# Single gate/value steps in token halves, quarter outputs copied by VectorE, and a bare group ahead of its score units, in an attention and SwiGLU kernel

## The chip, the core and the metric

The kernel runs on one core of a Trainium2 chip. The core has a matmul engine (TensorE, PE in the profile, with its weight loads shown as PEld), a vector engine (VectorE, DVE), an activation engine (ScalarE, ACT), a general engine (GpSimd, POOL) and a queue engine (SyncE, SP). They run in parallel, each works through its own list of instructions in order, and they wait for one another with semaphores. Matmul results go to PSUM, which has eight banks of 512 float32 columns in each of 128 partitions; everything else lives in SBUF. The metric is the device time of one execution in microseconds. The kernel before takes 429.18 us (median of three runs, 428.72 to 429.24).

## What is computed

Multi-head softmax attention over 8 batches, 12 heads, 448 tokens and 64 elements per head, then a gated feed-forward block over the 3584 resulting tokens:

```python
scores = scale * np.matmul(q, k.transpose(0, 1, 3, 2))
scores = scores - np.max(scores, axis=-1, keepdims=True)
attn = np.exp(scores)
attn = attn / (np.sum(attn, axis=-1, keepdims=True) + 1e-09)
out = np.matmul(attn, v)
...
g = x @ w_gate                              # 768 -> 1536
silu = g * (1.0 / (1.0 + np.exp(-g)))
val = x @ w_val                             # 768 -> 1536
return (silu * val @ w_out)                 # 1536 -> 768
```

Inputs and the output are float32; the matmuls run in float16.

## The kernel before

**Attention.** Two heads make a pair (48 pairs, six per batch). The scores of a pair come in units: a unit is a pair of score products for a slab of up to 128 keys against 448 queries, one product per head, in one PSUM tile `s` of two banks (`qk_quad`, L356 and L368), and one exponential on ScalarE that takes both heads from PSUM to SBUF (`exp`, L378, 128x896). From pair 12 on, a pair has three units of 128 keys and shares a fourth unit, which holds the 64 leftover keys of two pairs, with its neighbour. The weighted sums of values (L462, `acc`) take 8 matmuls that read the leftover keys (`pv_rest`, 64 rows) and 24 that read 128 keys (`pv_piece`), twelve for each head of the pair; each head has an `acc` tile of its own. VectorE closes a head with a reciprocal (L504) and a product (L505, `xt`); DMA transposes (L555, L561) then put the result into the feed-forward input `X`.

**Feed-forward.** Tokens go through it in blocks of 384 or 512. One *step* computes 128 of the 1536 inner columns for a block: six gate matmuls into `gp`, six value matmuls into `vp` (both L615), on ScalarE a tanh (L642, `sg`), on VectorE `t = (sg + 1) * gp` (L670) and `hts = t * vp` (L676). Outputs of a block come in *groups* (`OutPair.wide`, seven products of six matmuls, L734, with sums made beforehand by VectorE at L598 to L601) or, for what a group can't take, in *quarter outputs* (`plain_out`: twelve matmuls of 192 columns, L710, and a copy from PSUM at L717). The last two token blocks of 896 use another scheme (L888, L1082, L734), from about 278 us to the end.

**The order by hand.** The program is written in visits: a list `plan` gives each visit three score units and, in most visits, one pair whose values are due (`todo`). From the visit numbered `base` on, the table `VISITS` says what feed-forward work joins: (begins a block, steps, groups, quarter outputs, sums). A visit without `todo` is called bare. Visits with one step and a pair due (`lone`) are the *single steps*; there are seventeen of them, eight with 384 tokens and nine with 512. Their order on TensorE is: three score units, the eight leftover-key matmuls, the twelve of head 0 (`pv_side(p0, 0)`), the gate's six matmuls, the twelve of head 1, six value matmuls for the first half of the tokens, six for the second half. Visits with two steps, groups or quarter outputs stand between them. In single steps of 384 tokens the exponential of the third unit is held back (`late_exp`) until the tanh has been queued.

**PSUM.** Two pools use all eight banks. `ps_s` has three slots of two banks, tag "s": score tiles, the gate's tile, the group's `og` and some small outputs. `ps_f` has two slots of one bank, tag "f": `acc`, `vp`, `op`, `ob`. A new tile gets the slot that was released first, and its first matmul waits until the last reader of the old tile is done. In a single step of before, the gate's result `gp` is one bank of a `ps_s` tile, and the other bank (`self.spare`) takes the value product of the first token half; that of the second half is a `ps_f` tile. The slot is thus held until L676 has read the first half:

```python
gs = ps_s.tile([128, 2, 512], FP32, tag="s", name="gp")
gp, self.spare = gs[:, 0], gs[:, 1]
...
dst = ps_f.tile([128, 512], FP32, tag="f", name="vp") if half else self.spare
```

**Around the change.** In the last visits (`VISITS` entries 25 to 32) four quarter outputs, two groups and the sums of tokens and weights for the last scheme (`token_sums`, L1071 to L1074; `weight_sums`, L851 to L854 on GpSimd) are spread over the visits. The second of these groups falls into the bare visit (entry 31); there, two score units come ahead of the group and the third between its products.

Of the kernel before, what the change touches and what calls it, by code (L numbers as in the profile page):

```python
# [10 lines left out]
FP32 = mybir.dt.float32  # L11
# [54 lines left out]
def kernel(  # L66
# [410 lines left out]
    def pv_piece(pr, c, hx, first=False, last=True):  # L477
        for j in range(KR + 1):
            pv_mm(pr, hx, c, j, accs[pr][hx], first and c + j == 0, last and c == KR - 1 and j == KR)
# [19 lines left out]
    def pv_close(pr, hx):  # L499
        e_done(pr, hx)  # L500
        xt = Xts[pr % NX].rearrange("p (s h) d -> p s h d", h=2)
        a4 = accs[pr][hx][:, 0 : (KR + 1) * (D + 1)].rearrange("p (s d) -> p s d", s=KR + 1)
        r = attp.tile([128, KR + 1], FP32, tag="R", bufs=4, name="R")
        nc.vector.reciprocal(r[:], a4[:, :, D])  # L504
        nc.vector.tensor_tensor(  # L505
            xt[:, :, hx],
            a4[:, :, 0:D],
            r[:].unsqueeze(2).to_broadcast([128, KR + 1, D]),
            ALU.mult,
        )  # L510
# [3 lines left out]
            for c in range(KR):  # L514
                pv_piece(pr, c, hx)

    def pv_side(pr, hx):
        for c in range(KR):
            pv_piece(pr, c, hx)
        pv_close(pr, hx)  # L520

    def pv_quad(pr):
        pv_pieces(pr)
        if pr == XPE:
# [79 lines left out]
    class Step:  # L604
# [42 lines left out]
        def value(self, half):  # L647
# [14 lines left out]
                self.vp = ps_f.tile([128, 512], FP32, tag="f", name="vp")  # L662
            self.group("v", self.vp, range(half * NCB // 2, (half + 1) * NCB // 2))

        def gated(self):
            if self.t1 is None:
                n = self.at[2]
                self.t1 = fp.tile([128, 512], FP32, tag="t1", name="t1")
                self.readers.append(
                    nc.vector.scalar_tensor_tensor(  # L670
                        self.t1[:, 0:n], self.sg[:, 0:n], 1.0, self.gp[:, 0:n], ALU.add, ALU.mult
                    )
                )
# [12 lines left out]
    def store(osb, kk, l0, n, m0, w, queues=(nc.sync,), large_first=False):  # L686
# [12 lines left out]
        for x, (_, dst, src) in enumerate(parts):  # L699
            queues[x % len(queues)].dma_start(dst, src)  # L700

    def plain_out(kk, c0, hts, ch, m0, w, osb):
        if out_small[0]:
            out_small[0] = False
            op = ps_s.tile([128, 2, 512], FP32, tag="s", name="op")[:, 0]
        else:
            op = ps_f.tile([128, 512], FP32, tag="f", name="op")
        oh, off = divmod(m0, OH)
        for fb in range(NFB):
            nc.tensor.matmul(  # L710
                op[:, 0:w],
                lhsT=hts[:, fb, ts(ch, 128)],
                rhs=wo[oh][:, fb, ds(off, w)],
                start=fb == 0,
                stop=fb == NFB - 1,
            )
        nc.scalar.activation(osb[:, ds(m0, w)], op[:, 0:w], AF.Copy, scale=1.0 / HS)  # L717
        if m0 + w == DM:
            store(osb, kk, c0 + ch * 128, 128, 0, DM)

# [19 lines left out]
    def apart(mms, *others):  # L740
        for mm in mms:
            for other in others:
                tc.declare_no_dep(mm.ins, other.ins, reason="another bank")

    class OutPair:
# [29 lines left out]
        def wide(self, keep, add_sum, ns=(1, 2, 1), units=()):  # L775
            osb = self.open()
            g = ps_s.tile([128, 2, 512], FP32, tag="s", name="og")
            a, c = g[:, 0, 0:OH], g[:, 1, 0:OH]
            if self.last:
                bs = ps_s.tile([128, 2, 512], FP32, tag="s", name="ob")  # L780
                parts = [(i * QW, QW, bs[:, i, 0:QW]) for i in range(2)]
            else:
                parts = [(0, OH, ps_f.tile([128, 512], FP32, tag="f", name="ob")[:, 0:OH])]
            p1, p15 = (k[:, 0:OH] for k in keep)
            both = (nc.sync, nc.scalar)

            def products(lhs, m, first=False):
                return [(lo, w, b, product(b, lhs, self.tt(m, lo, w), first)) for lo, w, b in parts]

            def combine(dst, x, scale, y, lo, w):  # L790
                return nc.vector.scalar_tensor_tensor(  # L791
                    dst[:, ds(lo, w)], x[:, ds(lo, w)] if scale == HS else x, scale, y, ALU.mult, ALU.add
                )

            product(a, self.hh(0, self.x), self.bb(0, 0, 0, OH), True)
            keep1 = nc.scalar.activation(p1, a, AF.Copy, scale=1.0 / HS)
            apart(product(c, self.hh(0, self.y), self.tt(0, 0, OH), True), keep1)
            for unit in units:
                qk(*unit)
            done = [nc.vector.scalar_tensor_tensor(p15, c, 1.0 / HS, p1, ALU.mult, ALU.add)]  # L800
            for lo, w, b, mms in products(self.hs(0), 1, True):
                done.append(combine(c, p15, HS, b, lo, w))
            add_sum(ns[0])
            apart(product(a, self.hh(1, self.x), self.bb(0, 1, 0, OH)), *done)
            left = nc.scalar.activation(osb[0][:, 0:OH], a, AF.Copy, scale=1.0 / HS)
            for one in done[1:]:
                tc.declare_no_dep(left.ins, one.ins, reason="another bank")
            if self.last:
                self.stored(0, 0, OH, both)
            for lo, w, b, mms in products(self.hs(1), 2):  # L810
                combine(osb[1][:, OH:], b, 1.0 / HS, p15[:, ds(lo, w)], lo, w)
            if self.last:
                self.stored(1, OH, OH, both)
            add_sum(ns[1])
            apart(product(c, self.hs(2), self.bb(1, 1, 0, OH)), left)
            nc.scalar.activation(osb[0][:, OH:], c, AF.Copy, scale=1.0 / HS)
            if self.last:
                self.stored(0, OH, OH, both)
            else:
                self.stored(0)  # L820
            ends = []
            for lo, w, b in parts:
                mms = product(b, self.hh(1, self.y), self.tt(3, lo, w))
                apart(mms, *ends)
                ends.append(combine(osb[1], b, 1.0 / HS, p1[:, ds(lo, w)], lo, w))
                if self.last:
                    self.stored(1, lo, w, both)
            if not self.last:
                self.stored(1)
            add_sum(ns[2])  # L830
# [146 lines left out]
    with tc.manual_schedule():  # L977
# [50 lines left out]
        def add_block(i, visits):  # L1028
# [36 lines left out]
        ]  # L1065

        def token_sums(x, w, t, eng=nc.vector):
# [54 lines left out]
        def run_steps(n):  # L1122
            for _ in range(n - 2):
                run_fv()
            if n > 1:
                run_pair()
            elif n:
                run_fv()
# [109 lines left out]
        for x, (chunks, todo) in enumerate(plan):  # L1238
# [12 lines left out]
            lone = nf == 1 and bool(todo) and not split  # L1251
            behind = []
            for n, (pr, c) in enumerate(ordered if x else []):
                if n == 2 and ng and not todo:
                    behind.append((pr, c, small))
                    continue
                if n == 2 and ordered[n] in quads:
                    rests = open_products(rests, small)
                late = n == 2 and not todo and c < NC and pr < QUAD and bool(fvq) and not fvq[0].at[1]
                late = late or n == 2 and lone and not fvq[0].at[1]  # L1260
                qk(pr, c, small, late)
# [29 lines left out]
            for _, p0 in todo:  # L1291
                if split:
                    pv_split(p0)
                elif lone:
                    step = fvq.pop(0)
                    step.split = step.alone = True
                    gate_small[0] = False
                    pv_side(p0, 0)
                    step.gate()
                    pv_side(p0, 1)  # L1300
                else:
                    pv(p0)
                if p0 < XPE:
                    turns.append(p0)
                elif fvq and fvq[0].at[0] < p0 // NHP // NB - 1:
                    held.append(p0)
                else:
                    turn_x(p0)
# [25 lines left out]
            else:  # L1334
# [3 lines left out]
                for _ in range(ng):  # L1338
                    run_group(behind)
                if lone:  # L1340
                    step.gated()
                    step.value(0)
                    step.finish()
                    add_sum()
                elif bare_next(x):
                    for _ in range(nf):
                        run_fv()
                else:
                    run_steps(nf)
                for _ in range(no):  # L1350
                    run_o()
                    out_small[0] = True
# [159 lines left out]
```

## Time and profile before

The profiled execution took 428.64 us; its span from first to last instruction is 426.9 us. A visit of the single-step stage lasts 4.0 us (384 tokens) or 4.6 us (512).

| stretch (us) | what runs | length | PE busy | DVE busy | ACT busy | POOL busy |
|---|---|---|---|---|---|---|
| 123.50 to 245.10 | all single steps, with groups and two-step visits | 121.60 | 119.48 | 73.86 | 78.10 | 92.19 |
| 245.10 to 277.90 | visits with quarter outputs and groups, to the end of attention | 32.80 | 31.95 | 23.87 | 23.56 | 12.98 |
| whole span | | 426.9 | 418.5 | 265.4 | 247.5 | 224.3 |

The granted TensorE clock is 0.999 of full speed over the run. A busy PE is not PE at its peak: a matmul's row lasts from its start to its modelled end, some 0.15 to 0.2 us after the next one can start, so that short waits between matmuls hide under the tails of earlier rows. They are seen in the distance between the starts of rows that do the same work.

### The profile page before, as it was taken

The page shows a single profiled execution, that of the slowest core. Times are in us where ns is not written, and L with a number is a line of the kernel's source. Part 1 is how long each engine was busy: PE and PEld are TensorE (multiplying, and loading weights), DVE is VectorE, ACT ScalarE, POOL GpSimd, SP SyncE. Part 2 cuts the span into 40 slices and gives each one's busy share as a digit, 9 for nine tenths or more (in the row PEclk, how much of TensorE's full clock was granted, in tenths as well). Part 3 has the DMA queues.
Part 4 walks back from the last instruction along what each step waited for, and adds up shares of the span by engine and source line. Part 5 has one row for each costly group of instructions (what it writes and reads, how often), then busy time and mean ns, then how long its engine had stood idle before and what let it go on. Part 6 is the DMA issues. An engine that isn't in the chain of part 4 may idle for free.

```text
span 426.9 us, 10560 instructions
## 1 busy us (share of the span) xinstructions
PE 418.5 (98%) x4226; PEld 251.1 (59%) x4226; DVE 265.4 (62%) x592; ACT 247.5 (58%) x371; POOL 224.3 (53%) x343
## 2 busy tenths in 40 slices
PE   8999999999999999999999999999999999999996
PEld 3666666655556666675666577555555655555564
DVE  4667562786677664567655576665656575575563
ACT  6976667646767574766656677655543225545221
POOL 8656625987998777486967723599900000000000
PEclk9999999999999999999999999999999999999999
DMA  9999999999999999999999928410000331000125
GB/s 134 191 200 200 199 175 189 130 178 190 181 175 135 155 202 174 134 165 148 128 142 173 113 55 139 126 52 0 2 0 20 92 98 53 2 0 0 38 74 149
DMA packets 108465, 50.26 MB, mean 118 GB/s; under 512 B 60416, under 2 KB 105344, under 8 KB 108416
## 3 DMA queue, kind: packets, MB, share of 16 engines
q0 software_dynamic: 46800, 24.56, 48.4%
q1 hardware_dynamic: 61344, 24.79, 32.3%
q8 instruction: 33, 0.54, 0.5%
q10 hardware_dynamic: 272, 0.25, 0.2%
q14 instruction: 16, 0.13, 0.1%
HBM read 49.55 MB, written 11.01 MB: 142 GB/s over the span
## 4 chain that ended last, share of the span: by engine, by line
PE 90%; DVE 6%; ACT 2%; issue 1%; DVEq 0%; ACTq 0%
PE gp L615 15%; PE un L888 13%; PE og L734 10%; PE ub L888 10%; PE acc L462 8%; PE ob L734 8%; PE vp L615 7%; PE s L356 5%; PE op L710 4%; PE s L393 2%; PE acc L426 2%; DVE t L670 2%; PE op L1082 2%; DVE hts L676 2%; DVE xt L505 1%; PE tp L324 1%
## 5 line engine op out<-in xcount | busy, mean ns | idle before, releaser
L378 ACT ACTIVATE E<-s 128x896 f16<-128x896 f32 x126 | 107.4, 918 | 40.4 <-PE s L356 28.9
L615 PE MATMUL gp<-X,wg 128*128 128x384 f16 (+1 forms) x288 | 61.4, 353 | 0.1
L240 POOL COPY qk<-qkraw 128x512 f16<-128x512 f16 x70 | 43.6, 668 | 28.3 <-DMA qkT<-qk 25.4
L180 POOL DMA_DIRECT2D vraw<-in_v_dram x72 | 44.1, 634 | 14.6 <-DMA wo<-in_moe_w_out_dram 7.8
L615 PE MATMUL vp<-X,wv 128*128 128x384 f16 (+3 forms) x288 | 48.7, 305 | 0.0
L615 PEld LDWEIGHTS <-wv 128*128 128x128 f16 x432 | 39.5, 98 | 15.4
L462 PEld LDWEIGHTS <-E 128*128 128x128 f16 (+2 forms) x1224 | 40.3, 98 | 13.3 <-issue 5.4
L462 PE MATMUL acc<-vo,E 128*128 128x65 f16 (+2 forms) x1224 | 46.2, 193 | 0.6 <-DVE osb L791 0.3
L180 POOL DMA_DIRECT2D qkraw<-in_k_dram x70 | 42.5, 624 | 5.3 <-DMA wo<-in_moe_w_out_dram 3.4
L403 ACT ACTIVATE E<-s 112x896 f16<-112x896 f32 x48 | 40.7, 917 | 7.7 <-PE s L393 7.7
L670 DVE SCALAR_TENSOR_TENSOR t<-sg,gp 128x384 f32<-128x384 f32 (+1 forms) x48 | 29.4, 617 | 24.1 <-ACT sg L642 24.1
L615 PEld LDWEIGHTS <-wg 128*128 128x128 f16 x288 | 25.9, 97 | 21.8 <-issue 1.7
L734 PEld LDWEIGHTS <-hts 128*128 128x128 f16 x270 | 26.0, 98 | 16.6 <-issue 0.6
L642 ACT ACTIVATE sg<-gp 128x384 f32<-128x384 f32 (+1 forms) x48 | 26.0, 547 | 15.4 <-PE gp L615 13.7
L356 PE MATMUL s<-qkT 64*64 64x448 f16 (+1 forms) x288 | 31.7, 355 | 1.9 <-DVE hts L676 1.3
L505 DVE TENSOR_TENSOR xt<-acc,R 128x256 f16<-128x256 f32 x72 | 30.6, 425 | 2.5
L203 POOL DMA_DIRECT2D qkraw<-in_q_dram x43 | 29.4, 683 | 5.0 <-DMA vraw<-in_v_dram 2.0
L504 DVE RECIPROCAL R<-acc 128x4 f32<-128x4 f32 x72 | 12.9, 179 | 27.9 <-PE acc L462 27.7
L676 DVE SCALAR_TENSOR_TENSOR hts<-t,vp 128x384 f16<-128x384 f32 (+3 forms) x48 | 23.9, 499 | 3.0 <-PE vp L615 1.2
L953 ACT ACTIVATE silu<-un 128x448 f32<-128x448 f32 x24 | 13.0, 543 | 21.9 <-PE un L888 19.6
L937 DVE TENSOR_TENSOR un<-ub,kept 128x448 f32<-128x448 f32 x24 | 15.1, 631 | 16.6 <-ACT kept L934 10.3
L734 PE MATMUL og<-wo,hts 128*128 128x384 f16 x132 | 25.0, 326 | 0.4 <-ACT E L378 0.4
(207 smaller groups left out, 735.4 us busy)
## 6 DMA issues: line engine op xcount, KB each, us to landing
vraw<-in_v_dram POOLq DMA_DIRECT2D x72, 64.0 KB, 5.0
qkraw<-in_q_dram POOLq DMA_DIRECT2D x39, 112.0 KB, 4.6
qkraw<-in_k_dram POOLq DMA_DIRECT2D x68, 64.0 KB, 4.8
wg<-in_moe_w_gate_dram POOLq DMA_DIRECT2D x8, 288.0 KB, 10.0
wv<-in_moe_w_val_dram POOLq DMA_DIRECT2D x8, 288.0 KB, 10.5
wo<-in_moe_w_out_dram POOLq DMA_DIRECT2D x2, 1152.0 KB, 17.9
out_dram<-osb SPq DMA_DIRECT2D x7, 288.0 KB, 3.5
out_dram<-osb SPq DMA_DIRECT2D x9, 192.0 KB, 3.4
```

The lines of the kernel that those rows point to most:

```text
L180: eng.dma_start(dst[ts(s, 64)], rows)
L240: nc.gpsimd.tensor_copy(dst.rearrange("p c h d -> p h c d"), src)
L356: nc.tensor.matmul(s[ts(half, m), hx, 0:S].rearrange("p (c q) -> p c q", q=P), lhsT=t[ts(hx, 64), ds((c + low(pr, hx)) * 128 + half * m, m ...
L378: nc.scalar.activation(e, s[:, :, 0:S], AF.Exp, scale=sm_scale)
L403: nc.scalar.activation(e[:, :, 0:S], s[0:P, :, 0:S], AF.Exp, scale=sm_scale)
L462: nc.tensor.matmul(acc[ds(lo, m), ts((j + pr % 2) % (KR + 1), D + 1)], lhsT=e[rows, ds(hx * S + j * 128 + lo, m)], rhs=Vts[pr % NV][rows, ...
L505: nc.vector.tensor_tensor(xt[:, :, hx], a4[:, :, 0:D], r[:].unsqueeze(2).to_broadcast([128, KR + 1, D]), ALU.mult,)
L615: nc.tensor.matmul(dst[:, 0:w], lhsT=wslice(kind, self.fb, cb), rhs=X[kk][:, cb, ds(c0 + lo, w)], start=(cb == 0), stop=(cb == NCB - 1),)
L670: nc.vector.scalar_tensor_tensor(self.t1[:, 0:n], self.sg[:, 0:n], 1.0, self.gp[:, 0:n], ALU.add, ALU.mult)
L676: nc.vector.scalar_tensor_tensor(self.hts[:, self.fb, ds(lo, w)], self.t1[:, ds(lo, w)], 0.5 * HS, vp[:, 0:w], ALU.mult, ALU.mult)
L734: nc.tensor.matmul(dst, lhsT=lhs(n), rhs=rhs(n), start=first and n == 0, stop=n == NH - 1, skip_group_check=True)
L888: mm = nc.tensor.matmul(dst, lhsT=lhs[:, n], rhs=rhs[:, n], start=first and n == 0, stop=n == NK - 1, skip_group_check=True,)
```

## The change

Four things change.

1. Single steps run in a new method `halves`. The pair's values are finished first (`pv`, both heads, then both closings). Then the gate runs as two groups of six matmuls, one per token half, each in a bank of its own of one `ps_s` tile; each half has its own tanh and its own `t`. The held-back exponential is queued after both. The two value halves get a `ps_f` tile each, and `hts` is made from the two after both products. `pv_side` goes.
2. In quarter outputs from `base` on, VectorE copies the result from PSUM instead of ScalarE.
3. In a bare visit with a group, all three score units are handed to the group: its first two products come ahead of the first two units, and the third follows after the fourth product.
4. The table's last rows move: quarter outputs in entries 25, 26, 27 and 29 instead of 25, 26, 28 and 29; the group of entry 27 goes to entry 28; the sums ask for 1, 1, 2, 0, 1, 1 in entries 25 to 30 instead of 2, 2, 0, 2, 0, 0.

```diff
+        def halves(self):
+            w = self.at[2] // 2
+            parts = [ds(i * w, w) for i in range(2)]
+            gs = ps_s.tile([128, 2, 512], FP32, tag="s", name="gp")
+            self.sg = fp.tile([128, 512], FP32, tag="sg", name="sg")
+            self.t1 = fp.tile([128, 512], FP32, tag="t1", name="t1")
+            readers = []
+            for i, part in enumerate(parts):
+                g = gs[:, i, 0:w]
+                apart(self.group("g", gs[:, i], range(NCB), (i * w, w)), *readers)
+                readers.append(nc.scalar.activation(self.sg[:, part], g, AF.Tanh, scale=0.5))
+                readers.append(
+                    nc.vector.scalar_tensor_tensor(self.t1[:, part], self.sg[:, part], 1.0, g, ALU.add, ALU.mult)
+                )
+            while late_exp:
+                late_exp.pop(0)()
+            vps = [ps_f.tile([128, 512], FP32, tag="f", name="vp") for _ in parts]
+            for i, vp in enumerate(vps):
+                self.group("v", vp, range(NCB), (i * w, w))
+            for i, vp in enumerate(vps):
+                self.close(i * w, w, vp)
...
-        nc.scalar.activation(osb[:, ds(m0, w)], op[:, 0:w], AF.Copy, scale=1.0 / HS)
+        if by_vector[0]:
+            nc.vector.tensor_scalar_mul(osb[:, ds(m0, w)], op[:, 0:w], 1.0 / HS)
+        else:
+            nc.scalar.activation(osb[:, ds(m0, w)], op[:, 0:w], AF.Copy, scale=1.0 / HS)
...
-            for unit in units:
+            for unit in units[:2]:
                 qk(*unit)
...
+            for unit in units[2:]:
+                qk(*unit)
             for lo, w, b, mms in products(self.hs(1), 2):
...
-            (4, 0, 0, 1, 2), (0, 0, 0, 1, 2), (0, 0, 1, 0, 0), (0, 0, 0, 1, 2), (0, 0, 0, 1, 0),
-            (0, 0, 0, 0, 0), (0, 0, 1, 0, 0), (0, 0, 0, 0, 0),
+            (4, 0, 0, 1, 1), (0, 0, 0, 1, 1), (0, 0, 0, 1, 2), (0, 0, 1, 0, 0), (0, 0, 0, 1, 1),
+            (0, 0, 0, 0, 1), (0, 0, 1, 0, 0), (0, 0, 0, 0, 0),
...
-                if n == 2 and ng and not todo:
+                if ng and not todo:
                     behind.append((pr, c, small))
                     continue
...
-                elif lone:
-                    step = fvq.pop(0)
-                    step.split = step.alone = True
-                    gate_small[0] = False
-                    pv_side(p0, 0)
-                    step.gate()
-                    pv_side(p0, 1)
                 else:
                     pv(p0)
...
                 if lone:
-                    step.gated()
-                    step.value(0)
-                    step.finish()
+                    fvq.pop(0).halves()
                     add_sum()
...
+                by_vector[0] = True
                 for _ in range(no):
                     run_o()
```

More of the change, by code (lines that the diff above doesn't have):

```diff
@@ L515, in pv_pieces @@
                 pv_piece(pr, c, hx)
[L517 to L520, printed above, removed]
     def pv_quad(pr):
@@ L700, in store @@
             queues[x % len(queues)].dma_start(dst, src)
+    by_vector = [False]
     def plain_out(kk, c0, hts, ch, m0, w, osb):
```

## The prediction

> **What bounds the kernel now.** I first read the page for the busy shares. TensorE (PE) is busy nearly all the time, so only PE's waits can be won and only what makes PE wait can lose.
>
> ```profile
> PE 418.5 (98%) x4226; PEld 251.1 (59%) x4226; DVE 265.4 (62%) x592; ACT 247.5 (58%) x371; POOL 224.3 (53%) x343
> ```
>
> Next the stretches: in the stage of single steps the other engines have room (columns: stretch, length, then busy us of PE, PEld, DVE, ACT, POOL).
>
> ```profile
> 123.50:245.10 121.60, 119.48 (x1445) 77.52 (x1444) 73.86 (x197) 78.10 (x106) 92.19 (x154) 1.00 1.21 151
> ```
>
> Then the timeline of PE alone. A row's duration runs past the start of the next matmul, so I read distances between starts. First a visit behind a two-step visit, then single steps of 384 (from 183.28) and 512 tokens (191.97).
>
> ```profile
> 137.16 0.74 PE L356 MATMUL s<-qkT 64*128 64x448 f16 x6
> 137.74 0.76 PE L462 MATMUL acc<-vo,E 64*128 64x65 f16 x20
> 138.53 1.14 PE L615 MATMUL gp<-X,wg 128*128 128x384 f16 x6
> ...
> 183.28 0.55 PE L356 MATMUL s<-qkT 64*128 64x448 f16 x4
> 184.01 0.36 PE L356 MATMUL s<-qkT 64*128 64x448 f16 x2 [0.18 <-DVE hts L676]
> 184.20 0.82 PE L462 MATMUL acc<-vo,E 64*128 64x65 f16 x20
> ...
> 191.97 0.98 PE L356 MATMUL s<-qkT 64*128 64x448 f16 x6
> 192.77 0.89 PE L462 MATMUL acc<-vo,E 64*128 64x65 f16 x20
> 193.50 1.46 PE L615 MATMUL gp<-X,wg 128*128 128x512 f16 x6
> 194.79 0.53 PE L462 MATMUL acc<-vo,E 128*128 128x65 f16 x12
> 195.16 0.82 PE L615 MATMUL gp<-X,wv 128*128 128x256 f16 x6
> 195.81 0.82 PE L615 MATMUL vp<-X,wv 128*128 128x256 f16 x6
> ```
>
> Three units of scores take 0.58 us where nothing holds them (137.16 to 137.74), but 0.92 (183.28) and 0.80 (191.97) behind a single step: the third unit waits 0.34 or 0.22 us. The row at 184.01 names the cause: the third `s` tile needs the slot that held the gate, and L676 reads its spare bank last. The twenty `acc` matmuls ahead of the gate take 0.59 us unhindered (24 + 8 take 0.96 from 245.71 to 246.67, less 0.37 for twelve, 194.79 to 195.16); at 192.77 they take 0.73, waiting 0.14 us for the second half's L676. At 137.74 they take 0.79: there the gate itself waits 0.20 us, for a score slot whose exponential isn't done.
>
> Last, the same for ACT and DVE in one visit of 512 (scores start at 196.56, next ones at 201.15).
>
> ```profile
> 196.97 2.54 ACT L378 ACTIVATE E<-s 128x896 f16<-128x896 f32 x3 [1.38 <-PE s L356]
> 199.58 0.60 ACT L642 ACTIVATE sg<-gp 128x512 f32<-128x512 f32 x1
> 200.51 0.68 DVE L670 SCALAR_TENSOR_TENSOR t<-sg,gp 128x512 f32<-128x512 f32 x1
> 201.29 0.42 DVE L676 SCALAR_TENSOR_TENSOR hts<-t,gp 128x256 f16<-128x256 f32 x1
> 201.63 0.41 DVE L676 SCALAR_TENSOR_TENSOR hts<-t,vp 128x256 f16<-128x256 f32 x1
> ```
>
> The chain gate, tanh, t, L676 ends at 201.71 for the slot, 0.56 us into the next visit.
>
> **What the change removes.** (1) *The third unit's wait.* The gate's slot is free after the second t instead of after L676. By hand for 512 tokens, from the start of scores: scores, leftovers and both heads 1.53 (245.14 to 246.67), gate halves 0.655 each (195.16 to 195.81), to 2.84; value halves to 4.15; the next scores at 4.25, with 0.09 for the change of matmul form. ACT starts at 0.41 and is through three exponentials at 2.85 (0.815 us apart, as in 2.54 for three); the first tanh starts then, the second at 3.13, ending 3.51; the second t ends at 3.97. The slot is wanted at 4.64. For 384: gate halves end at 2.03 and 2.52, the second tanh ends at 3.05, the second t at 3.45; scores come at 3.60, the slot is wanted at 3.81. The held-back exponential now starts at about 2.96 and ends at 3.87; its slot is wanted last, at 3.99. So no wait: eight visits of 0.32 to 0.34 (2.6 us) and nine of 0.20 to 0.22 (1.9), 4.5 us in all.
> (2) *The wait of the leftover matmuls* for the second half's L676 at these seventeen places: nearly 0.14 us each after 512 tokens, less after 384, 1.1 us in all. Afterwards that L676 no longer queues behind a late t: it starts 0.11 us into the next visit (a result is read 0.2 us after its last matmul, as L504 at 195.36 after the twelve that end at 195.16) and ends, 0.42 us long, with 0.05 us to reach PE, at 0.58, just when the `acc` tile is wanted (0.58). After 384 tokens it is 0.07 earlier. This margin is zero for nine visits, so I put back a wait of between 0 and the old one: 0.05 x 9 = 0.45, bounds 0 and 1.1.
> (3) *The gate's own wait*: three of 0.20 us after two-step visits (137.74, 176.02, 207.96) and three of 0.07 after groups, 0.8 us. The gate now comes 0.37 us later, behind head 1.
>
> **What it adds.** *PE*: six more matmuls in each of seventeen steps. Six of 256 columns take 0.655 us, twelve 1.310, six of 512 take 1.295 (193.50 to 194.79 with nothing between); so +0.015 each, +0.26 us. The weight load stays hidden: value halves of this width already run at that pace. The Trainium skill, TensorE: Matmul & The Clock Gate, section Back-to-back issue gap, says otherwise: in a stream of weight loads and matmuls some 131 ns per matmul at 512 columns and 81 at 128. By a line between these (98 ns at 256, my estimate) a gate would cost 0.39 us more, 6.6 us in all. The rows of this trace, 216 and 109 ns, disagree, and I go by them.
> *ACT*: a tanh of 192 or 256 columns isn't in the trace; bounds are the copy of 128x192 (0.346) and the tanh of 128x384 (0.495). Even the upper one twice, with 2.54 of exponentials, is 3.5 of a 3.6 us visit. *DVE*: two t of 0.35 or 0.42 (by L676 of the same width) for one of 0.55 or 0.68. Behind them in DVE's queue stand L676, a sum (0.55), the V copy (0.29) and the next closings (1.18, 252.10 to 253.28): 3.3 us of 3.6, or 3.5 of 4.25. Covered; without cover each 0.1 us costs 1.7 us over the stage. Closing both heads together gives the value tiles their slots at about 2.2 and 2.8, and they are wanted at 2.84 and 3.50 (2.52 and 3.02 for 384). SP's transposes wait for the same closings, now earlier for head 1; no DMA is added. POOL's queue isn't changed.
>
> **The tail.** Four copies leave ACT (0.35 each) for DVE, where no such row exists: between the V copy (0.29) and L676 of 192 columns (0.35) at best, 0.42 at worst; taken 0.35. There ACT sets waits of 0.1 to 0.2 us in scores (247.75, 261.97, 264.73); on DVE the copy stands ahead of the V copy (needed two visits later) and the sum, and its slot is wanted by the third score unit. In the bare visit the group waited for exponentials:
>
> ```profile
> 266.97 0.38 PE L356 MATMUL s<-qkT 64*64 64x448 f16 x4
> 267.78 1.14 PE L734 MATMUL og<-wo,hts 128*128 128x384 f16 x6 [0.43 <-ACT E L378]
> ...
> 271.32 0.56 DVE L791 SCALAR_TENSOR_TENSOR og<-p,ob 128x384 f32<-128x384 f32 x1 [0.30 <-PE ob L734]
> 272.10 1.14 PE L734 MATMUL ob<-E,hsum 128*128 128x384 f16 x6
> ```
>
> That wait (0.61) and 0.26 before it go. But the product at 272.10 needs the L791 above it, done at 271.88, only 0.22 earlier. One sum (0.55) is now queued ahead of it, so DVE may be next: then the product comes 0.35 later than before instead of 0.8 earlier. With up to 0.1 for each copy: -0.8 to +0.75; the DVE rows there are slow ones (two V copies in 1.72, L1072 in 1.56), so I take -0.2.
>
> **Sum.** -4.5 - 1.1 - 0.8 + 0.26 + 0.45 - 0.2 = -5.9 us. Against the profiled execution's 428.64 (span 426.9 and 1.7 around it) that is 422.7; the median of the runs shown is 0.54 above that execution, so 423.3, and I say 423.2. The last stage (from 278 us) I leave as it is: the weight sums that it waits for start from releases by PE and move with it.
>
> **Rivals.** *New small waits* (0.14): the leftovers' wait stays (+0.65 beyond what I put back), the held-back exponential is late by 0.1 in eight visits (+0.8; margin 0.12) and the tail goes to its upper end (+0.95). About -3.5: 425.7. For: margins are that thin. Against: each is positive by rows.
> *The wait only changes its name* (0.03): score slots wait for exponentials in place of L676, so 4.5 us stay, -1.4: 427.8. For: ACT's late tanh after 512 tokens. Against: slots free 0.5 us early by the sum above.
> *Narrow matmuls cost more* (0.02): for no change the twelve would have to lose 0.35 us per step, 29 ns each; 195.16 to 195.81 excludes it for value halves. 429.0. The rule of the Trainium skill named above (TensorE: Matmul & The Clock Gate) would put the time here too.
> *DVE becomes the bound* (0.08), the other side: between closings and the next leftovers. Slow rows exist: V copies of 0.85 where GpSimd works beside it (245.58) and a sum of 1.07 (128.94). With both in every visit DVE needs 3.3 + 1.1 = 4.4 us for 384 tokens and 4.6 for 512; before a visit took 4.0 and 4.6. That is 8 x 0.4 = +3.2, the other gains lost: 432.4. It decides from 4.0 us of DVE per visit. Against: the V copies between 120 and 250 us have a median of 0.287.
>
> **How the numbers follow.** The forecast has 0.73. This measurement can tell about 0.2% (0.9 us) from no change. Faster: 0.73 + 0.14 + 0.03 = 0.90; same 0.02; slower 0.08. The likeliest one's own range is 421.6 to 424.9; down to 421.2 if the zero margins and the tail fall well, and up to 427.0 over the small waits, leaving out under 0.2.
>
> **What would show it.** Right: in single-step visits the three score units take 0.58 to 0.60 us from first start to first leftover matmul, visits last 3.6 and 4.25 us, and tanh and t come in pairs of 192 or 256 columns. PE's rows from 278 us on come some 6 us earlier. Wrong: scores that still take 0.8, leftover matmuls that wait for L676, a gate half slower than 0.655 (512) or 0.495 (384), or DVE without gaps in the stage. The bare visit's fifth product waiting on L791 would show the tail's upper end.

## The result, and the profile after

The changed kernel takes 427.67 us (median of seven runs, 426.87 to 428.34), the kernel before 428.9 us beside it: a ratio of 0.997, 95% interval 0.9959 to 0.9982. That is 1.2 us less, where 5.9 us less were forecast; 427.67 lies above the range. A second measurement (below) gave the same, 0.9975.

The busy shares and the two stretches of the profiled execution after (stage of single steps, and from there to the last stage; columns as before):

```profile
PE 416.5 (98%) x4328; PEld 258.8 (61%) x4328; DVE 268.7 (63%) x613; ACT 247.9 (58%) x384; POOL 224.8 (53%) x343
```

```profile
124.00:243.25 119.25, 118.00 (x1549) 85.83 (x1548) 75.45 (x214) 79.47 (x123) 93.10 (x157) 1.00 1.21 156
243.25:277.00 33.75, 31.69 (x467) 21.47 (x467) 25.25 (x60) 22.68 (x29) 14.27 (x16) 1.00 0.57 107
```

The stage went from 121.62 us (123.52 to 245.14) to 119.24, 2.4 less; the stretch behind it, the tail, from 32.71 (245.14 to 277.85) to 33.76, 1.05 more. Together that is 1.3 us, about what the medians show. The profiled execution itself, the slowest of the seven, is only 0.3 us faster: its stage begins 0.48 us later, and from its first `un` matmul, with which the last stage begins, to the end of its stores it takes 149.60 us where the kernel before took 149.05, 0.55 more. The profile of the second measurement has neither (stage from 123.24, last stage 148.96 us), so I take both for differences between runs.

PE's timeline behind single steps of the two widths. The visit of 384 tokens runs from 182.54 to 186.45, that of 512 from 191.03 to 195.55:

```profile
182.54 1.04 PE L356 MATMUL s<-qkT 64*128 64x448 f16 x6
183.41 1.13 PE L462 MATMUL acc<-vo,E 64*128 64x65 f16 x32
184.38 1.15 PE L610 MATMUL gp<-X,wg 128*128 128x192 f16 x12
185.37 1.15 PE L610 MATMUL vp<-X,wv 128*128 128x192 f16 x12
186.45 0.38 PE L368 MATMUL s<-qkT 64*64 64x448 f16 x4
...
191.03 0.74 PE L356 MATMUL s<-qkT 64*128 64x448 f16 x6
191.61 1.39 PE L462 MATMUL acc<-vo,E 64*128 64x65 f16 x32
192.83 1.47 PE L610 MATMUL gp<-X,wg 128*128 128x256 f16 x12
194.14 1.47 PE L610 MATMUL vp<-X,wv 128*128 128x256 f16 x12
195.55 0.74 PE L356 MATMUL s<-qkT 64*128 64x448 f16 x6
```

Read the distances between starts. With 512 tokens the three score units now take 0.58 us (191.03 to 191.61), as forecast, but the leftovers and both heads behind them take 1.22 for 0.96 unhindered: the wait stands there now. With 384 tokens the scores still take 0.87 (182.54 to 183.41). Visits last 3.91 and 4.52 us, not 3.6 and 4.25. The gate's matmuls behave as forecast: 0.99 us for twelve of 192 columns, 1.31 for twelve of 256, and nothing waits ahead of them (183.41 to 184.38 is 0.97).

What ACT waited for in the stage tells the rest (us in all, times, longest):

```profile
ACT sg L670 <- DVE t L672: 8.2, 16, 0.5
```

and the rows of one visit, ACT's and then DVE's:

```profile
186.17 3.34 ACT L378 ACTIVATE E<-s 128x896 f16<-128x896 f32 x4
189.35 0.43 ACT L670 ACTIVATE sg<-gp 128x256 f32<-128x256 f32 x1
190.33 0.38 ACT L670 ACTIVATE sg<-gp 128x256 f32<-128x256 f32 x1 [0.55 <-DVE t L672]
191.43 2.54 ACT L378 ACTIVATE E<-s 128x896 f16<-128x896 f32 x3 [0.72 <-PE s L356]
```

```profile
189.82 0.42 DVE L672 SCALAR_TENSOR_TENSOR t<-sg,gp 128x256 f32<-128x256 f32 x1 [0.48 <-ACT sg L670]
190.75 0.42 DVE L672 SCALAR_TENSOR_TENSOR t<-sg,gp 128x256 f32<-128x256 f32 x1 [0.51 <-ACT sg L670]
191.09 0.74 DVE L693 SCALAR_TENSOR_TENSOR hts<-t,vp 128x256 f16<-128x256 f32 x2
```

The second tanh (190.33) waits for the first `t` (189.82), and the second `t` (190.75) for the second tanh: four instructions in a row across two engines. Yet the second tanh needs nothing that the first `t` makes. `halves` takes the order away between the matmuls of the second half and the first half's readers (`apart`), but not between the second tanh and the first `t`, which work on the same tiles, `gs` and `sg`, in other columns; there the scheduler kept them in program order. (Which of the two tiles made it do so isn't shown.) In the tail, PE now waits 1.54 us in the bare group:

```profile
269.34 0.38 PE L356 MATMUL s<-qkT 64*64 64x448 f16 x4
271.26 1.14 PE L756 MATMUL ob<-E,hsum 128*128 128x384 f16 x6 [1.54 <-DVE og L813]
272.23 1.14 PE L756 MATMUL og<-wo,hsum 128*128 128x384 f16 x6
```

### The profile page after: what moved, and what is told of

Read it like the earlier page. It is cut to its first block, busy times and chain, and to the rows that moved or that the text cites. A ratio compares the mean times of both kernels' runs of the same rounds, so it can differ in the third digit from the quotient of the medians.

```text
span 426.6 us, 10831 instructions
## 1 busy us (share of the span) xinstructions
PE 416.5 (98%) x4328; PEld 258.8 (61%) x4328; DVE 268.7 (63%) x613; ACT 247.9 (58%) x384; POOL 224.8 (53%) x343
## 4 chain that ended last, share of the span: by engine, by line
PE 89%; DVE 4%; DMA 2%; POOL 2%; ACT 1%; issue 1%; ACTq 0%; DVEq 0%; POOLq 0%
PE gp L610 14%; PE un L912 13%; PE vp L610 11%; PE ub L912 10%; PE og L756 9%; PE acc L462 8%; PE ob L756 7%; PE s L356 5%; PE op L729 4%; PE acc L426 2%; PE op L1106 2%; PE s L393 2%; DMA qkraw<-in_k_dram 2%; PE s L368 1%; POOL qkraw L203 1%
## 5 line engine op out<-in xcount | busy, mean ns | idle before, releaser
L610 PE MATMUL gp<-X,wg 128*128 128x256 f16 (+3 forms) x390 | 61.7, 304 | 0.0
L610 PE MATMUL vp<-X,wv 128*128 128x256 f16 (+3 forms) x390 | 58.6, 293 | 0.0
L240 POOL COPY qk<-qkraw 128x512 f16<-128x512 f16 x70 | 44.2, 678 | 24.9 <-DMA qkT<-qk 23.2
L462 PEld LDWEIGHTS <-E 128*128 128x128 f16 (+2 forms) x1224 | 38.6, 98 | 10.4 <-issue 5.8
L462 PE MATMUL acc<-vo,E 128*128 128x65 f16 (+2 forms) x1224 | 43.3, 193 | 1.3 <-DVE hts L693 0.3
L610 PEld LDWEIGHTS <-wg 128*128 128x128 f16 x390 | 34.3, 98 | 16.4 <-issue 2.0
L687 DVE SCALAR_TENSOR_TENSOR t<-sg,gp 128x384 f32<-128x384 f32 (+1 forms) x31 | 18.7, 617 | 22.8 <-ACT sg L637 22.8
L505 DVE TENSOR_TENSOR xt<-acc,R 128x256 f16<-128x256 f32 x72 | 30.5, 424 | 2.5
L693 DVE SCALAR_TENSOR_TENSOR hts<-t,vp 128x256 f16<-128x256 f32 (+3 forms) x65 | 29.1, 468 | 3.2 <-PE vp L610 1.2
L356 PE MATMUL s<-qkT 64*64 64x448 f16 (+1 forms) x288 | 30.5, 355 | 0.6 <-DVE osb L737 0.2
L965 DVE TENSOR_TENSOR kept<-ub,kept 128x448 f32<-128x448 f32 x24 | 15.0, 624 | 15.0 <-PE ub L912 15.0
L221 DVE COPY vo<-vraw 128x512 f16<-128x512 f16 (+1 forms) x48 | 20.3, 425 | 4.2 <-DMA vraw<-in_v_dram 4.1
```

What stands on the lines that cost most here:

```text
L240: nc.gpsimd.tensor_copy(dst.rearrange("p c h d -> p h c d"), src)
L356: nc.tensor.matmul(s[ts(half, m), hx, 0:S].rearrange("p (c q) -> p c q", q=P), lhsT=t[ts(hx, 64), ds((c + low(pr, hx)) * 128 + half * m, m ...
L462: nc.tensor.matmul(acc[ds(lo, m), ts((j + pr % 2) % (KR + 1), D + 1)], lhsT=e[rows, ds(hx * S + j * 128 + lo, m)], rhs=Vts[pr % NV][rows, ...
L505: nc.vector.tensor_tensor(xt[:, :, hx], a4[:, :, 0:D], r[:].unsqueeze(2).to_broadcast([128, KR + 1, D]), ALU.mult,)
L610: nc.tensor.matmul(dst[:, 0:w], lhsT=wslice(kind, self.fb, cb), rhs=X[kk][:, cb, ds(c0 + lo, w)], start=(cb == 0), stop=(cb == NCB - 1),)
L693: nc.vector.scalar_tensor_tensor(self.hts[:, self.fb, ds(lo, w)], self.t1[:, ds(lo, w)], 0.5 * HS, vp[:, 0:w], ALU.mult, ALU.mult)
```

## The experiments

The table gives ratios to the kernel before, which was measured again beside each group of runs (428.52 to 428.94 us), and stage, tail and last stage of each profiled execution, in us, worked out from the starts of PE's rows (first scores of the stage, first scores ahead of the first quarter output, first `un` matmul, end of the span). Kernels that were measured at different times are best compared by their ratios.

| kernel | median us | ratio (95%) | stage | tail | last stage |
|---|---|---|---|---|---|
| before | 428.9 | 1 | 121.62 | 32.71 | 149.05 |
| changed | 427.67 | 0.997 (0.9959-0.9982) | 119.24 | 33.76 | 149.60 |
| e1 second tanh free | 424.68 | 0.9898 (0.9881-0.9915) | 115.36 | 34.15 | 149.53 |
| e2 part 1 alone | 427.92 | 0.9975 (0.996-0.9989) | 119.19 | 33.42 | 149.61 |
| e3 parts 2 to 4 alone | 429.8 | 1.0019 (1.0007-1.0031) | 121.61 | 33.52 | 148.98 |
| e4 changed, sum earlier | 427.25 | 0.9956 (0.9941-0.9972) | 119.18 | 32.35 | 149.50 |
| e5 free, old tail | 423.26 | 0.9877 (0.9862-0.9892) | 115.86 | 33.68 | 149.30 |
| e6 free, sum earlier | 422.43 | 0.9854 (0.9841-0.9867) | 115.33 | 32.37 | 149.32 |
| e7 as e6, copies on ACT | 422.4 | 0.9852 (0.9838-0.9865) | 115.45 | 32.37 | 149.54 |
| e8 second unit's sums out | 428.32 | 0.9993 (0.9983-1.0003) | 119.17 | 33.52 | 150.49 |
| e9 third and fourth's out | 426.92 | 0.9962 (0.9947-0.9977) | 119.19 | 31.93 | 149.71 |
| e10 as e6, token sum earlier | 422.56 | 0.985 (0.9836-0.9865) | 115.35 | 31.94 | 149.43 |
| e11 changed again | 427.7 | 0.9975 (0.9965-0.9985) | 119.46 | 33.53 | 148.96 |
| e12 changed, tail as in e10 | 426.54 | 0.9937 (0.9922-0.9951) | 119.19 | 31.93 | 149.81 |

**e1: the second tanh need not wait for the first `t`.**

```diff
-                readers.append(nc.scalar.activation(self.sg[:, part], g, AF.Tanh, scale=0.5))
+                tanh = nc.scalar.activation(self.sg[:, part], g, AF.Tanh, scale=0.5)
+                apart([tanh], *readers[1:])
+                readers.append(tanh)
```

> The changed kernel, with one order taken away: the second half's tanh no longer has to come behind the first half's t (they read different banks and write different columns). Theory: this order is what kept the gain small. Behind it the second tanh of a 192-column half starts 0.48 us late (row at 152.94) and of a 256-column half 0.55 us late (194.79); without it the held-back exponential of the eight visits of 384 tokens starts that much earlier and the third score unit's wait of about 0.21 us goes (8 x 0.21 = 1.7 us), and after 512 tokens hts is ready in time, so the leftover matmuls' waits of 0.07 to 0.30 us (1.3 us over the stage) go. That makes 427.67 - 3.1 = 424.6 us, with score units that take 0.58 us from first start to first acc in all single-step visits. Rival (the wait changes its name): the first tanh stands behind three exponentials after 512 tokens and sets the pace, or score slots wait for exponentials; then at most 1 us is won, 426.7 to 427.7, and the third unit or the acc matmuls still wait for ACT.

424.68 us, where the theory had 424.6. PE's and ACT's rows of the same visits:

```profile
180.63 0.74 PE L356 MATMUL s<-qkT 64*128 64x448 f16 x6
181.21 1.12 PE L462 MATMUL acc<-vo,E 64*128 64x65 f16 x32
182.16 1.15 PE L610 MATMUL gp<-X,wg 128*128 128x192 f16 x12
183.15 1.15 PE L610 MATMUL vp<-X,wv 128*128 128x192 f16 x12
184.24 0.38 PE L368 MATMUL s<-qkT 64*64 64x448 f16 x4
...
188.51 0.74 PE L356 MATMUL s<-qkT 64*128 64x448 f16 x6
189.09 1.12 PE L462 MATMUL acc<-vo,E 64*128 64x65 f16 x32
190.05 1.47 PE L610 MATMUL gp<-X,wg 128*128 128x256 f16 x12
191.36 1.47 PE L610 MATMUL vp<-X,wv 128*128 128x256 f16 x12
192.76 0.74 PE L356 MATMUL s<-qkT 64*128 64x448 f16 x6
```

```profile
182.86 0.33 ACT L670 ACTIVATE sg<-gp 128x192 f32<-128x192 f32 x1
183.35 0.33 ACT L670 ACTIVATE sg<-gp 128x192 f32<-128x192 f32 x1 [0.16 <-PE gp L610]
183.58 0.91 ACT L378 ACTIVATE E<-s 128x896 f16<-128x896 f32 x1
```

Scores take 0.58 in both, leftovers and heads 0.95 and 0.96, visits 3.61 and 4.25 us. The second tanh starts 2.72 us after the scores (183.35), as the forecast had it, and the held-back exponential follows at 2.95. Against the kernel before, the stage gives 6.26 us. The rival falls: in these visits nothing takes the wait's place. That the total is so near the theory's is partly luck: against the changed kernel the stage gives 3.88 us, more than the 3.1 expected, and the tail takes 0.39 back (33.76 to 34.15).

**e2 and e3: the parts by themselves.** e2 keeps part 1 and restores the tail of before; e3 restores the single steps of before and keeps parts 2 to 4.

> Part 1 alone: single steps by halves, with the copies, the bare group's order and the table's last rows as before. Theory: the stage of single steps gives the 2.4 us that the profile of the changed kernel shows (121.62 to 119.24), and the stretch behind it stays at its 32.7 us of before: 428.9 - 2.4 = 426.5 us. Rival: the 1.05 us that the changed kernel lost behind the stage come from the stage itself (an earlier arrival that meets later operands), not from parts 2 to 4; then 427.5 us, with 33.7 us behind the stage.

> Parts 2 to 4 alone: copies on DVE, the bare group's order, the table's last rows; single steps as before. Theory: these lose 1.05 us behind the stage, because the bare group's fifth product waits some 1.5 us for DVE (sum, V copies and token sum ahead of its combine): 428.9 + 1.05 = 429.9 us, with a row of 1.4 to 1.7 us of waiting for L813's counterpart. Rival: the loss needs the earlier arrival of the stage; then 428.9 us or, by my original sum, 428.7.

e2: the stage gave its 2.4 us, but the time is the rival's, only 1.0 us less: the old tail, met 2.6 us earlier, costs 0.7 us more. PE waits there twice for closings, which come late behind two DVE rows (L596 and L1093) of about double length:

```profile
262.17 0.88 PE L356 MATMUL s<-qkT 64*128 64x448 f16 x6
263.40 0.20 PE L462 MATMUL acc<-vo,E 64*128 64x65 f16 x1 [0.35 <-DVE xt L505]
263.94 1.13 PE L462 MATMUL acc<-vo,E 64*128 64x65 f16 x31 [0.35 <-DVE xt L505]
```

```profile
259.56 0.55 DVE L595 TENSOR_TENSOR hsum<-hts 128x768 f16<-128x768 f16 x1
260.15 1.15 DVE L596 TENSOR_TENSOR hsum<-hts,hsum 128x768 f16<-128x768 f16 x1
261.23 1.56 DVE L1093 TENSOR_TENSOR vraw<-X 128x1344 f16<-128x1344 f16 x1
```

Before, the same two rows took 0.56 and 0.85 us. e3 lost 0.86 us where the theory had 1.05; its profile has the wait in the bare group, 1.5 us for the combine, as the theory said. So both halves of the change cost some 0.7 to 0.8 us in the tail, and together 1.05 (0.82 in e11's profile), not the sum.

**e4: one sum earlier.** In the table, `(0, 0, 0, 1, 1), (0, 0, 0, 0, 1)` of entries 29 and 30 become `(0, 0, 0, 1, 2), (0, 0, 0, 0, 0)`.

> The changed kernel with one number pair of the table altered: the sum that entry 30 asks for (L596, 1.26 us at 267.32) is asked for by entry 29, ahead of the closings and the two V copies of the last visits. Theory: DVE is what the bare group's fifth product waits for, so taking 1.26 us of its queue away brings that product 1.2 us earlier: 427.67 - 1.2 = 426.5 us, and its wait falls from 1.54 to about 0.35 us. Rival: DVE is late there for another reason (the V copies wait for their data, or GpSimd's work slows the rows wherever they stand); then the wait stays above 1 us and the time within 0.4 us of 427.7.

The profile shows the theory's gain: the wait falls from 1.54 to 0.4 us and the tail from 33.76 to 32.35. The time shows less of it: 427.25, runs from 426.64 to 428.74. I come back to the difference at e12.

**e5, e6, e7: the second tanh free, with three tails.** e5 has the tail of before, e6 the changed one with e4's edit, e7 is e6 without `by_vector[0] = True`.

> Single steps by halves with the second tanh free, and the copies, the bare group's order and the table's last rows of the kernel before. Theory: the stage gives 6.3 us as in the run with the second tanh free (115.36 for 121.62), and the old tail, met earlier, loses 0.7 us as it did with part 1 alone (33.42 for 32.71), by DVE rows that GpSimd slows: 428.9 - 6.3 + 0.7 = 423.3 us. Rival: with the stage 6 us earlier the old tail collides more (weight sums on GpSimd wait for transfers, not for PE, and so move against it): 424.3 us or more.

> The changed kernel with the second tanh free and the sum of entry 30 asked for by entry 29. Theory: both corrections add, 424.7 - 1.4 (the stretch behind the stage went from 33.76 to 32.35 with the sum moved) = 423.3 us. Rival: behind a faster stage DVE's slow rows fall elsewhere and take it back: 424.0 to 424.7 us.

> As the run before it (second tanh free, sum moved), and the four quarter copies on ACT again (part 2 undone). Theory: on DVE the copy is late where GpSimd works beside it (PE waited 0.58 us for it at 245.51 with the second tanh free, 0.1 to 0.4 us at other scores of the changed kernel), on ACT it costs waits of 0.1 to 0.2 us; so about 0.5 us less than with the copies on DVE, 422.8 us. Rival: ACT's queue (three exponentials ahead of the copy) gives the same waits: within 0.3 us of the run before it.

e5 came at 423.26 for 423.3 (by its ratio 423.6): stage and tail add. e6 was better than expected, 422.43 for 423.3: 1.9 us less than e1 by the ratios, 1.8 by the tails. For e7 the rival held: where the quarter copies run makes no difference here (422.40). What parts 3 and 4 are worth with the sum moved is e5 less e7, 0.9 us.

**e8 and e9: is it GpSimd that makes DVE's rows long?** Both leave weight sums out and point the units that would read them to the first ones' tensors, so their output is another: e8 where `weight_sums` is called, e9 by an early return in it.

> The changed kernel without the second unit's four weight sums on GpSimd (the unit reads the first unit's instead, so its part of the output is another). GpSimd then rests from about 265.5 us to the last stage. Theory: DVE is late for the bare group because its rows there run beside GpSimd's: V copies, L596 and L1096 took 1.73, 1.26 and 1.56 us and should take about 0.48, 0.55 and 0.85, so that the product's wait of 1.54 us for the combine ends: 427.67 - 1.5 = 426.2 us. Rival: those rows are slow for their own operands (reads that fall on one part of the memory, late data) wherever GpSimd stands: rows and wait unchanged, 427.6 us.

> The changed kernel without the weight sums of the third and fourth unit on GpSimd (those units read the first two units' instead, so their part of the output is another). These are the six rows of GpSimd that stood beside DVE's slow rows before the bare group (264 to 269 us in the run with the second unit's sums out, which took out the wrong ones). Theory: DVE's rows are slow because GpSimd works beside them; V copies, L596 and L1096 fall from 1.73, 1.26 and 1.56 us to about 0.5, 0.55 and 0.85, the product's wait of 1.54 us for the combine ends, and the stretch behind the stage falls from 33.76 to about 32.2 us, a ratio to the kernel before of about 0.9935. Rival: the rows are slow for their own operands; rows, wait and ratio (0.997) as in the changed kernel.

e8 missed its aim: the sums that run beside the bare group are the third and fourth unit's (GpSimd's rows at 264.26 to 269.06 stayed), and so did DVE's rows and the wait of 1.54. Its time, by the ratios 0.8 to 1.0 us above the changed kernel's, I can't explain; its profile has 5.18 us from the last matmul to the end, where the changed kernel's two profiles have 4.32 and 3.75. e9 aimed right. GpSimd's rows there in the changed kernel, which e9 doesn't have:

```profile
265.42 0.91 POOL L877 TENSOR_TENSOR E<-wg,wg 128x384 f16<-128x384 f16 x1
266.29 0.96 POOL L878 TENSOR_TENSOR E<-wg,E 128x384 f16<-128x384 f16 x1
267.21 0.96 POOL L875 TENSOR_TENSOR E<-wv 128x384 f16<-128x384 f16 x1
268.25 1.11 POOL L876 TENSOR_TENSOR E<-E,wv 128x384 f16<-128x384 f16 x1
```

DVE's rows ahead of the combine, in the changed kernel and then in e9 (where L1096 has become L1098):

```profile
265.68 1.73 DVE L221 COPY vo<-vraw 128x512 f16<-128x512 f16 x2
267.32 1.26 DVE L596 TENSOR_TENSOR hsum<-hts,hsum 128x768 f16<-128x768 f16 x1
268.51 1.56 DVE L1096 TENSOR_TENSOR vraw<-X,vraw 128x1344 f16<-128x1344 f16 x1
269.99 0.54 DVE L822 SCALAR_TENSOR_TENSOR p<-og,p 128x384 f32<-128x384 f32 x1
```

```profile
265.16 0.48 DVE L221 COPY vo<-vraw 128x512 f16<-128x512 f16 x2
265.56 0.55 DVE L596 TENSOR_TENSOR hsum<-hts,hsum 128x768 f16<-128x768 f16 x1
266.02 0.85 DVE L1098 TENSOR_TENSOR vraw<-X,vraw 128x1344 f16<-128x1344 f16 x1
266.79 0.55 DVE L822 SCALAR_TENSOR_TENSOR p<-og,p 128x384 f32<-128x384 f32 x1
```

The same rows in the same order take 2.7 us less from the first to the last start (4.31 to 1.63), the product's wait is gone, and the tail falls to 31.93. The cause of the long rows is shown by the rows. The time alone would not show it: 0.9962 was measured for 0.9935, and its interval holds the rival's 0.997 but not the theory's number.

**e10: the second token sum one visit earlier too.** `in (5, 3, 2, 1)` becomes `in (5, 4, 2, 1)`, on e6.

> Second tanh free, the sum of entry 30 moved to entry 29, and the second token sum (L1096 of the changed kernel, 1.56 us ahead of the bare group's combine) put one visit earlier, ahead of the closings. Theory: the 0.54 us that the bare group's fifth product still waits for DVE (264.69 in the run without this step) goes: 422.4 - 0.5 = 421.9 us, ratio about 0.984. Rival: the closings behind it come 0.85 us later and something waits for them (the turned tiles of the last visit, or the V copies): 422.4 us or more, ratio 0.9854 or above.

The tail falls to 31.94 as in e9, with the copies alone left beside GpSimd; the time can't be told from e6's (0.985 and 0.9854), and its interval holds both expectations. So the last 0.4 us are seen in the profile only.

**e11 and e12: the changed kernel again, beside one with both tail edits.**

> The changed kernel again, beside the run below on the same chip: a ratio of about 0.997 as the first time; the comparison of the two is what is asked.

> The changed kernel with its sum of entry 30 and its second token sum one visit earlier, and the order of the second tanh left as it is. Theory: what the changed kernel loses behind the stage is DVE's late combine, and 1.8 us come back (33.76 to 31.9 us): 1.8 us less than the changed kernel beside it, ratio about 0.9928. Rival: with the second tanh still held, half or more of it is lost again elsewhere, as the times with the sum moved (0.9956) and with the sums beside left out (0.9962) suggest, though their profiles showed the whole gain: at most 0.8 us less than the changed kernel, ratio 0.995 or above.

e12 is 1.2 us under e11 (426.54 and 427.70), between the two expectations; its interval holds the theory's 0.9928, and the rival's 0.995 at its edge. The profiled tails differ by 1.6 us, and yet both profiled executions have a span of 425.2 us: e12's stage begins 1.03 us later (124.27 against 123.24), and from its last matmul to the end it takes 0.82 us more (4.57 against 3.75). These two places move without any edit: the two profiles of the changed kernel differ there by 0.76 and 0.57 us. The matmuls between, from the first `un` to the last, take 145.25 us in both. So the profiles hold the tail's gain in full; whether the medians lose part of it by more than such scatter stays open.

The best kernels, e6, e7 and e10, take 422.4 to 422.6 us: 6.1 to 6.2 us less than before and some 5 less than the changed kernel.

## Why the prediction was wrong

**The step that failed** is in part (1) of "What the change removes": "The first tanh starts then, the second at 3.13, ending 3.51; the second t ends at 3.97", and "the second tanh ends at 3.05" for 384 tokens. I priced the second tanh by when its matmuls and ACT are ready. It also waits for the first `t`: it started 3.76 us after the scores with 512 tokens (194.79 against 191.03, forecast 3.13) and 3.40 with 384 (185.94 against 182.54, forecast 2.72):

```profile
185.94 0.33 ACT L670 ACTIVATE sg<-gp 128x192 f32<-128x192 f32 x1 [0.48 <-DVE t L672]
194.79 0.38 ACT L670 ACTIVATE sg<-gp 128x256 f32<-128x256 f32 x1 [0.55 <-DVE t L672]
```

What follows it was priced with margins of 0.12 us and zero, so the visits came out 0.31 and 0.27 us longer than forecast. By distances between starts, with e1's as the unhindered ones: behind steps of 384 tokens the held-back exponential came late, and the third unit kept 0.22 to 0.31 us of a wait of 0.34 to 0.36, 2.1 us in all eight visits. Behind steps of 512 the slot came in time but for 0.09 and 0.15 us in two visits; there `hts` came late, and in five of the seven visits that have leftovers these wait 0.21 to 0.34 us, where they waited 0.12 to 0.14. Of the signs of being wrong that were named, scores that still take 0.8 us, leftovers that wait, and the bare group's fifth product on its combine all came. Without that order (e1) the same sums give visits of 3.61 and 4.25 us against 3.6 and 4.25 forecast. The mechanism was right; one link of its chain was missing, and it stands in the list of what each instruction waits for, which the diff alone doesn't tell.

**The other terms of the stage.** The gate's own wait went, as forecast. Narrow matmuls cost what was forecast (1.31 us for twelve of 256, e1's as well): a matmul takes 216 ns at 512 columns, 109 at 256 and 82.5 at 192 (0.99/12), so half the width takes half the time. The Trainium skill (TensorE: Matmul & The Clock Gate, section Back-to-back issue gap) has 131 ns at 512 columns and, by my estimate on a line between its figures, 98 at 256. These rows disagree with it, and the 6.6 us that it asked for never came. Two workings are off without consequence: the rows listed for DVE add up to 3.4 and 3.7 us, not 3.3 and 3.5, and of the seventeen places in (2) four have no leftovers, as a bare visit follows. The 0.45 us put back for the zero margin were not needed: with the order gone the stage gave 6.26 us, against 5.69 with that term and 6.14 without.

**The tail** was forecast at -0.2, with bounds of -0.8 and +0.75; it was +1.05, and +0.82 in the second profile. I had the right chain (the bare group's fifth product behind the combine, a sum ahead of it) and quoted slow rows from it, but charged the added sum 0.55 us, its price where DVE is alone. It took 1.26, as it stood where GpSimd works (e9: 0.55 without GpSimd's rows). And I left out that the tail changes when the stage ends earlier: e2 shows 0.7 us of that without any change to the tail. The lower bound was real: e9, e10 and e12 stand at 0.78 below before.

**The rivals.** New small waits named all three places (held-back exponential, leftovers, tail) and forecast 425.7, too little at each: 0.22 to 0.31 us for 0.1 at the exponential, at most 0.34 for 0.14 at the leftovers, 1.05 for 0.75 in the tail. The wait only changing its name came closest in time (427.8), by luck: it left the tail as forecast, where the tail lost 1.05, and put 1.2 us on the stage (1.4 with the tail's 0.2), which gave 2.4. Its mechanism, ACT's late tanh, was half right: the tanh was late while ACT was free and kept waiting. DVE as the bound did not come: it was busy 75.45 of 119.25 us. Narrow matmuls that cost more did not come either.

## What to carry to other kernels

When one operation is split into halves so that two engines can overlap, write down for every new instruction all that it waits for, and count in the other instructions on the same tile, in other columns too. An order that the scheduler keeps between them costs as much as a true dependency, here some 0.5 us of waiting in each of sixteen steps and 3 us of time in all. A row's price belongs to the place it came from: a vector instruction that is moved beside another engine's work must be charged the longer row found there. And a stretch whose work is paced by transfers or by another engine is not the same stretch when it is reached three microseconds earlier.

## What the runs showed of the hardware

DVE rows between SBUF operands took 1.8 to 3.6 times as long where GpSimd's tensor sums ran beside them: 1.73 against 0.48 us for two V copies, 1.26 against 0.55, 1.56 against 0.85, with one set of GpSimd rows taken out (e9). It isn't tensor sums alone: in the stage of the changed kernel a sum at 148.41 took 1.08 us and a V copy at 201.21 took 0.70, both beside GpSimd's copies (L240). Rows that read PSUM did not slow: L505 at 264.79 took its usual 0.42 us while GpSimd's sum of 264.56 ran. GpSimd is slowed as well: two of its sums took 1.26 and 1.22 us beside e2's rows, and 0.91 with no such row beside them. In e10 the DVE row that began first (L1098 at 260.46) kept its 0.85 us, and GpSimd's sum of 260.51 took 1.57. The Trainium skill (SBUF — State Buffer, section SBUF: two separate sides) says that the two engines share one pair of ports that is held for a whole instruction while the other is blocked, for DVE instructions with two SBUF inputs or in a mode that uses both ports. The traces agree with waiting by turns: a DVE sum of 0.55 became 1.26, longer by 0.71, less than one GpSimd sum (0.91), and GpSimd's sum in e10 was longer by 0.66, less than the DVE row ahead of it (0.85).
